# Attention into a mixture of experts: one group's keys and queries loaded in two halves of the heads, six dummy matmuls fewer, and an uneven last output

## The chip, the cores and the metric

The kernel runs on one core of a Trainium2 chip. The time is device microseconds of one launch, as the median of several runs of the same program. The kernel before took 399.28 us (median of 4 runs, 398.71 to 399.73). A change of less than about 0.2% of that, 0.8 us, is treated as no change.

## The reference

```
# attention: B=4, H=8, S=768, D=64; heads 0, 2, 6 are "retrieval" heads
scores = q @ k^T / sqrt(D)
causal mask for retrieval heads; the others see the first 4 keys and a window of 64 keys
a = exp(scores) / (sum + 1e-9)
x = (a @ v), heads side by side, as [B*S, H*D] = [3072, 512]

# four experts, all applied to every row: w1 [4, 512, 1024], w2 [4, 1024, 512]
p = domain_probs / (sum + 1e-9)
out = sum over e of p[:, e] * (relu(x @ w1[e]) @ w2[e])       # [3072, 512], float32
```

All inputs are float32 in the chip's main memory. The kernel computes in float16 with float32 sums.

## The kernel before, in words

**Groups and units.** The 3072 rows are cut into 8 groups of 384 rows: one batch entry has two of them (c = 0 and c = 1). A group's attention makes `xT[g]`, its rows transposed, as four tiles of 128 features (`ct` = 0 to 3, two heads in each). `PLACE` puts head h into tile h % 4, upper or lower half. Then come four units, one for each expert e. A unit has a first layer (32 matmuls on L895: eight output tiles `ft`, each a sum over the four `ct`), a Relu for each `ft` on ScalarE (L908), and a second layer (24 matmuls on L919: three row tiles j, each a sum over eight `ft`), which VectorE scales by p and adds into `acc` (L931, L935).

**What sets the order.** The order on every engine is the order in which the program is written out; nothing is rearranged. While the units of group g are written out, steps of the attention of group g + 1 are slipped between them by the loop at the end of the kernel. It counts planned nanoseconds: attention of group 1 begins when the units of group 0 have `spent` more than `begin` = 1.15 units, and is then spread up to `end`. One unit is 10380 planned nanoseconds. In group 0 a first-layer step counts 0.6 of its time and a second-layer step 1.4, so the first layer of expert 1 begins at about 1.0 units.

**Group 0** has no earlier units to hide behind. Its attention runs first, in the first 22.4 us, with float32 transposes, and TensorE waits for other engines and loads in it. `warm_up` puts dummy matmuls on zeros into such waits (L388). Heads 5 and 7 come last. The last dummies, ten of 256 columns, stand ahead of the value matmuls of head 7. The first unit starts right behind these. For group 0 it takes the tiles in the order `cts` = (0, 2, 1, 3): tile 1 holds heads 1 and 5, tile 3 heads 3 and 7.

**Group 1** is loaded by `load_triples` into `k16` and `qt16`, one DMA for all eight heads of the keys and one for the queries. TensorE transposes both, two heads at a time: `transposes(hp)` is six matmuls for the queries and six for the keys (L516), each a step of its own in the loop. Pairs hp = 0 and 1 (heads 0 to 3) come before the scores, hp = 3 (heads 6, 7) behind the scores of heads 0 and 2, and hp = 2 (heads 4, 5) behind those of heads 1 and 3. From group 2 on, the transposes are done by DMA.

**The loads.** Nearly all loads of the first 65 us are issued by GpSimd (POOL): they convert float32 to float16 on the way. POOL works in program order. `landed(x)` is a tiny copy that makes POOL wait until a transfer has arrived. The order in the stretch that changes is: both halves of w1(1), wait for w1(0), k, q, wait for w2(0), w2(1), wait for q, the values of the three retrieval heads (`vR`), w1(2), wait for w2(1), two other heads' values (`vS`), w2(2), three more, wait for w1(2), w1(3), w2(3). The DMAs that POOL issues take eight semaphores in turn; each first waits until the one eight places before it has landed.

**The end.** The last row tile of the last expert is computed by `last_tile` in two parts of 256 columns, so that the first part is on its way out (issued by SyncE, SP) while the second is computed (its output is issued by ScalarE, ACT).

Of the kernel before, what the change touches and what calls it, by code (L numbers as in the profile page):

```python
# [17 lines left out]
def kernel(  # L18
# [33 lines left out]
    nc = tc.nc  # L52
    P = 128
    B, H, S, D = q.shape
    E, DM, F = moe_w1.shape
    CH = 3 * P
    NCH = S // CH
    N = B * S
    HP = H // 2
# [9 lines left out]
    RH = [h for h in range(H) if RETR[h]]  # L69
# [80 lines left out]
    def half(u):  # L150
        return slice(u * D, (u + 1) * D)
# [5 lines left out]
    def own_v(h):  # L157
        return half(PLACE[h][1])
# [10 lines left out]
    def v_tiles(b, c, h):  # L169

        if RETR[h]:
            return vR[b % 2][:, 3 * c : 3 * c + 3, RH.index(h), :]
        if b:
            return windows(vSf, c)[:, :, SH.index(h), :]
        return vS[:, c, :, SH.index(h), :]
# [10 lines left out]
    def rows_of(x, b, h, c):  # L186
        return x[b, h, c * CH : (c + 1) * CH, :].rearrange("(j p) d -> p j d", p=P)

    def tiles_of(x, b, h, c):
        return x[b, h, c * CH : (c + 1) * CH, :].rearrange("(t r) d -> r t d", r=TK)  # L190

    def windows_of(x, b, h, c):

        assert b > 0
        first = ((b * H + h) * S + c * CH - WO) * D
        return bass.AP(x.tensor, x.offset + first, [[D, P], [WQ * D, WT], [1, D]])
# [10 lines left out]
        q16[b, c] = att.tile([P, 3, H, D], FP16, name="q16", bufs=2)  # L207
        load_by_rows(q, q16[b, c], b, c)

    def load_triples(x, dst, b, c):  # L210

        gp.dma_start(
            out=dst.rearrange("p h j d -> p h (j d)"),
            in_=x[b, :, c * CH : (c + 1) * CH, :].rearrange(
                "h (p j) d -> p h (j d)", j=3
            ),
        )
# [47 lines left out]
    def load_v(b, c, heads):  # L265
        for h in heads:
            t = v_tiles(b, c, h)
            if RETR[h]:
                gp.dma_start(out=t[:, :, 0:D], in_=rows_of(v, b, h, c))  # L269
            elif b:  # L270
                gp.dma_start(  # L271
                    out=t[:, :, own_v(h)], in_=windows_of(v, b, h, c)
                )
            else:
                gp.dma_start(  # L275
                    out=t[R0:P, :, own_v(h)],
                    in_=tiles_of(v, b, h, c),
                )
# [18 lines left out]
    def load_w1(e, f0, f1):  # L297
        x = moe_w1[e].rearrange("(u c d) f -> u d c f", u=2, c=DMP)
        for u in range(2):
            gp.dma_start(  # L300
                out=w1sb[half(u), e * DMP : (e + 1) * DMP, f0:f1],
                in_=x[u, :, :, f0:f1],
            )
# [47 lines left out]
    for h in range(H):  # L351
        if h == 2:
            nc.sync.dma_start(
                out=v_s32, in_=v[0, :, 0:NS, :].rearrange("h r d -> r h d")
# [13 lines left out]
        eng = nc.scalar if h < HP else nc.sync  # L368
        eng.dma_start(out=q32[:, :, h, :], in_=rows_of(q, 0, h, 0))
    nc.sync.dma_start(  # L370
        out=probs, in_=moe_domain_probs.rearrange("(t p) e -> p t e", p=P)
# [14 lines left out]
    def warm_up(ps, n, cols):  # L386
        for _ in range(n):
            nc.tensor.matmul(  # L388
                out=ps[:, 0:cols], lhsT=warm[:, 0:P], rhs=warm[:, 0:cols],
                start=True, stop=True,  # L390
            )
# [63 lines left out]
    k16 = att.tile([P, H, 3, D], FP16, name="k16", bufs=1)  # L455
    qt16 = att.tile([P, H, 3, D], FP16, name="q16", bufs=2)

    def landed(x):

        gp.tensor_copy(out=seen, in_=x)  # L460

    def w1_of(e):
        return w1sb[D : D + 1, e * DMP, 0:1]

    def w2_of(e):
        return w2sb[0:1, e * FTP, 0:1]

    load_w1(1, 0, F)
    landed(w1_of(0))
    load_triples(k, k16, 0, 1)  # L470
    load_triples(q, qt16, 0, 1)
    landed(w2_of(0))
    load_w2(1)
    landed(qt16[0:1, 0, 0, 0:1])
    load_v(0, 1, RH)
    load_w1(2, 0, F)
    landed(w2_of(1))
    load_v(0, 1, SH[:2])
    load_w2(2)
# [12 lines left out]
    def mm_ns(cols):  # L492
        return cols / 2.4 + 2.5

    def attention(b, c):
        g = b * NCH + c
# [212 lines left out]
        def values(h):  # L709
            if RETR[h]:  # L710
                yield from values_r(h)
                return
            ct, u = PLACE[h]
            if first and u == 1:
                ps = pO.tile([P, 512], FP32, name="pO", bufs=2)
            else:
                ps = pV.tile([P, 512], FP32, name="pV", bufs=2)
            if first:
                warm_up(ps, {3: 4, 4: 4, 5: 6, 7: 10}.get(h, 0), 256)
            work = []  # L720
            for es, parts in es_of[h]:
                for t, o, q0, nq in parts:
                    work.append((es, t, o, q0, nq))
            ns = 0
            for n, (es, t, o, q0, nq) in enumerate(work):
                nc.tensor.matmul(  # L726
                    out=ps[:, q0 : q0 + nq],
                    lhsT=v_tile(b, c, h, t),
                    rhs=es[:, o : o + nq],
                    start=(n == 0),  # L730
                    stop=(n == len(work) - 1),
                    skip_group_check=True,
                )
                ns += mm_ns(nq)
                if ns > 300 and n < len(work) - 1:
                    yield ns
                    ns = 0

            r, o = half(u), half(1 - u)
            pair = first and h in (3, 4)  # L740
            if not pair or u == 0:
                rc_of[0] = att.tile([P, CH], FP32, name="rc", bufs=4)
            rc = rc_of[0]
            nc.scalar.activation(  # L744
                out=rc[r, :], in_=ps[o, 0:CH], func=AF.Ln, bias=eps[o, :]
            )

            def scale(r=r, ps=ps):
                nc.vector.tensor_tensor(  # L749
                    out=xT[g][r, ct, :], in0=ps[r, 0:CH], in1=rc[r, :], op=ALU.mult  # L750
                )

            if not pair:
                nc.scalar.activation(out=rc[r, :], in_=rc[r, :], func=AF.Exp, scale=-1.0)  # L754
                later(scale)
            elif u == 0:
                scale_of[0] = scale
            else:
                nc.scalar.activation(out=rc, in_=rc, func=AF.Exp, scale=-1.0)
                later(scale_of[0])  # L760
                later(scale)

            yield ns + (600.0 if g == 1 else 0.0)
# [92 lines left out]

    def last_tile(e, nt, hs, acc):

        for n, eng in enumerate((nc.sync, nc.scalar)):
            cols = slice(n * DM // 2, (n + 1) * DM // 2)  # L860
            ps = pV.tile([P, 512], FP32, name="pV", bufs=2)
            for ft in range(FTP):
                nc.tensor.matmul(
                    out=ps[:, 0 : DM // 2],
                    lhsT=hs[:, ft, 2 * P : 3 * P],
                    rhs=w2sb[:, e * FTP + ft, cols],
                    start=(ft == 0),
                    stop=(ft == FTP - 1),
                )
            nc.vector.scalar_tensor_tensor(  # L870
                out=acc[:, cols], in0=ps[:, 0 : DM // 2],
                scalar=p_sb[:, nt, e : e + 1], in1=acc[:, cols],
                op0=ALU.mult, op1=ALU.add,
            )
            eng.dma_start(out=out[nt * P : (nt + 1) * P, cols], in_=acc[:, cols])


    acc = {}
# [88 lines left out]
    UNIT = FTP * DMP * mm_ns(CH) + 3 * FTP * mm_ns(DM)  # L967
    for g in range(G):
        nxt = g + 1
        n_units = len(units[g])  # L970
        att_steps = iter(())
        if nxt < G:
            att_steps = attention(nxt // NCH, nxt % NCH)
        loads(g + 2)

        begin = {0: 1.15, 1: 1.0}.get(g, 0.0) * UNIT
        end = {0: 3.5}.get(g, 0.90 * n_units) * UNIT

        att_ns = 3500.0 if nxt % NCH == 0 else 5600.0
        if nxt < NCH:  # L980
            att_ns += 1100.0 + HP * 3 * 400.0 + NSH * 600.0
        spent = 0.0
        done = 0.0
        to_transpose = g + 2 < G
        for ns, share in moe_steps(units[g]):

            spent += ns * (share if g == 0 else 1.0)
            tick(ns)
            if to_transpose and spent > {0: 0.9, 1: 0.75}.get(g, 0.5) * n_units * UNIT:
                dma_transposes(*divmod(g + 2, NCH))  # L990
                to_transpose = False
            while done < (spent - begin) / (end - begin) * att_ns:
                step = next(att_steps, None)
                if step is None:
                    break
                done += step
                tick(step)
        for ns in att_steps:
            tick(ns)
        tick(LAG)  # L1000
# [35 lines left out]
```

The softmax here doesn't subtract the row's maximum and nothing guards it: scores larger than these inputs give would overflow.

## Time and profile before

| | |
|---|---|
| median of 4 runs | 399.28 us |
| the profiled execution: its own time, its span | 399.16 us, 397.4 us |
| TensorE (PE) busy | 389.0 us, 98% of the span |
| ScalarE, VectorE, GpSimd busy | 55%, 39%, 36% |
| granted TensorE clock, mean | 0.998 |
| TensorE idle just before it, longest: values of head 5 (load of vS) | 1.02 us |
| the same: second layer of expert 1 (load of w2) | 0.82 us |
| the same: values of head 6 (ScalarE's exp) | 0.76 us |
| POOL's wait for q of group 1 | 7.7 us |

How to read it: the profile is of one execution. Times run from the span's start. A line of the timeline gives the start, the length, the engine, the line of the kernel, the operation with the tiles that it writes and reads, the shape and the count; in brackets stands the idle time of the engine before it and what ended that. In the answers by windows each engine has its busy time and, in parentheses, its number of instructions; then come the granted clock (1.00 is full), the mean busy share of the 16 DMA engines, and GB/s. TensorE's matmuls are pipelined, so the end of one lies behind the start of the next; start-to-start times are the safer measure.

### The profile page before, as it was taken

The page shows a single profiled execution, that of the slowest core. Times are in us where ns is not written, and L with a number is a line of the kernel's source. Part 1 is how long each engine was busy: PE and PEld are TensorE (multiplying, and loading weights), DVE is VectorE, ACT ScalarE, POOL GpSimd, SP SyncE. Part 2 cuts the span into 40 slices and gives each one's busy share as a digit, 9 for nine tenths or more (in the row PEclk, how much of TensorE's full clock was granted, in tenths as well). Part 3 has the DMA queues.
Part 4 walks back from the last instruction along what each step waited for, and adds up shares of the span by engine and source line. Part 5 has one row for each costly group of instructions (what it writes and reads, how often), then busy time and mean ns, then how long its engine had stood idle before and what let it go on. Part 6 is the DMA issues. An engine that isn't in the chain of part 4 may idle for free.

```text
span 397.4 us, 7140 instructions
## 1 busy us (share of the span) xinstructions
PE 389.0 (98%) x2829; PEld 221.7 (56%) x2829; DVE 156.4 (39%) x344; ACT 219.2 (55%) x468; POOL 143.6 (36%) x184
## 2 busy tenths in 40 slices
PE   8899999999999999999999999999999999999996
PEld 5754566555555555555555555555555555555553
DVE  7734765324442234434332333433443223422222
ACT  3754569444766546655764446745564456853331
POOL 8833795908907806900049202940000000000000
PEclk9999999999999999999999999999999999999999
DMA  9999999999999999960779958990472000020002
GB/s 169 162 207 190 172 197 168 146 193 135 117 179 164 121 150 113 150 80 12 140 83 178 59 97 120 112 152 12 86 114 83 2 12 0 11 79 2 0 2 80
DMA packets 166133, 42.23 MB, mean 106 GB/s; under 512 B 156396, under 2 KB 161108, under 8 KB 166100
## 3 DMA queue, kind: packets, MB, share of 16 engines
q0 software_dynamic: 102656, 20.98, 63.1%
q1 hardware_dynamic: 61700, 20.27, 27.0%
q10 hardware_dynamic: 1744, 0.52, 0.6%
q8 instruction: 22, 0.36, 0.4%
q14 instruction: 11, 0.09, 0.1%
HBM read 43.57 MB, written 6.29 MB: 125 GB/s over the span
## 4 chain that ended last, share of the span: by engine, by line
PE 77%; DMA 15%; POOL 6%; issue 1%; DVE 0%; POOLq 0%
PE pA L895 35%; PE pO L919 35%; DMA w1sb<-in_moe_w_dram 4%; DMA w2sb<-in_moe_w_dram 4%; PE pA L614 4%; DMA q<-in_q_dram 3%; DMA kR<-kRr 2%; POOL vR L269 2%; PE pV L726 1%; PE pV L662 1%; DMA vS<-in_v_dram 1%; POOL w1sb L300 1%; POOL vS L275 1%; POOL vS L326 0%; POOL q L201 0%
## 5 line engine op out<-in xcount | busy, mean ns | idle before, releaser
L895 PE MATMUL pA<-xT,w1sb 128*128 128x384 f16 x1024 | 185.9, 326 | 0.1
L919 PE MATMUL pO<-w2sb,hs 128*128 128x512 f16 x760 | 179.0, 379 | 0.8 <-DMA w2sb<-in_moe_w_dram 0.8
L908 ACT ACTIVATE hs<-pA 128x384 f16<-128x384 f32 x256 | 122.0, 492 | 94.8 <-PE pA L895 89.5
L895 PEld LDWEIGHTS <-w1sb 128*128 128x128 f16 x1024 | 95.9, 98 | 59.6 <-issue 0.5
L919 PEld LDWEIGHTS <-hs 128*128 128x128 f16 x760 | 70.8, 98 | 73.9 <-DMA w2sb<-in_moe_w_dram 1.2
L632 ACT ACTIVATE es<-pA 128x384 f16<-128x384 f32 (+2 forms) x122 | 60.0, 511 | 53.6 <-PE pA L614 52.3
L935 DVE SCALAR_TENSOR_TENSOR acc<-pO,p_sb,acc 128x512 f32<-128x512 f32 x71 | 53.3, 751 | 71.7 <-PE pO L919 71.3
L227 POOL DMA_DIRECT2D kSr<-in_k_dram x30 | 30.1, 1008 | 31.9 <-DMA kS<-kSr 21.8
L223 POOL DMA_DIRECT2D kRr<-in_k_dram x18 | 14.2, 786 | 68.5 <-DMA kR<-kRr 68.4
L749 DVE TENSOR_TENSOR xT<-pV,rc 64x384 f16<-64x384 f32 x37 | 20.5, 554 | 32.0 <-ACT rc L754 24.3
L271 POOL DMA_DIRECT2D vS<-in_v_dram x30 | 30.6, 1030 | 0.0
L931 DVE TENSOR_SCALAR acc<-pO,p_sb 128x512 f32<-128x512 f32 x24 | 18.0, 751 | 28.8 <-PE pO L919 28.6
L636 DVE TENSOR_TENSOR es<-es,mC 128x256 f16<-128x256 f16 (+1 forms) x42 | 10.9, 259 | 45.3 <-ACT es L632 44.3
L744 ACT ACTIVATE rc<-pV,eps 64x384 f32<-64x384 f32 x37 | 21.3, 576 | 12.0 <-PE pV L726 11.5
L614 PE MATMUL pA<-qT,kR 128*128 128x384 f16 (+2 forms) x120 | 24.5, 279 | 0.7 <-ACT qT L525 0.4
L754 ACT ACTIVATE rc<-rc 64x384 f32<-64x384 f32 x38 | 19.8, 521 | 1.2
L269 POOL DMA_DIRECT2D vR<-in_v_dram x24 | 19.3, 806 | 0.4 <-issue 0.3
L636 DVE TENSOR_TENSOR es<-es,mW 128x384 f16<-128x384 f16 x30 | 10.7, 358 | 16.9 <-ACT es L632 16.8
L614 PEld LDWEIGHTS <-kR 128*128 128x128 f16 x120 | 11.4, 98 | 10.7 <-DVE kR L532 0.7
L726 PEld LDWEIGHTS <-vS 128*128 128x128 f16 x255 | 13.4, 98 | 6.9 <-DMA vS<-in_v_dram 1.3
L662 PEld LDWEIGHTS <-es 128*128 128x128 f16 x252 | 13.2, 97 | 7.2 <-ACT es L632 0.9
L614 PEld LDWEIGHTS <-kS 128*128 128x128 f16 x255 | 13.3, 98 | 6.6
(102 smaller groups left out, 190.5 us busy)
## 6 DMA issues: line engine op xcount, KB each, us to landing
out_dram<-acc SPq DMA_DIRECT2D x23, 256.0 KB
w1sb<-in_moe_w_dram POOLq DMA_DIRECT2D x8, 512.0 KB, 9.9
w2sb<-in_moe_w_dram POOLq DMA_DIRECT2D x4, 1024.0 KB, 13.3
kSr<-in_k_dram POOLq DMA_DIRECT2D x30, 112.0 KB, 3.7
vS<-in_v_dram POOLq DMA_DIRECT2D x30, 112.0 KB, 5.5
q<-in_q_dram POOLq DMA_DIRECT2D x18, 128.0 KB, 4.3
vR<-in_v_dram POOLq DMA_DIRECT2D x24, 48.0 KB, 4.6
kRr<-in_k_dram POOLq DMA_DIRECT2D x18, 48.0 KB, 3.5
```

The lines of the kernel that those rows point to most:

```text
L227: gp.dma_start(out=kSr[:, :, SH.index(h), own(h)], in_=windows_of(k, b, h, c),)
L269: gp.dma_start(out=t[:, :, 0:D], in_=rows_of(v, b, h, c))
L271: gp.dma_start(out=t[:, :, own_v(h)], in_=windows_of(v, b, h, c))
L614: nc.tensor.matmul(out=ps[:, o : o + nq], lhsT=key_tile(b, c, h, t), rhs=qTs[b, c][:, hp, q0 : q0 + nq], start=(n == 0 or not first), stop ...
L632: nc.scalar.activation(out=es[:, 0:cols], in_=ps[:, 0:cols], func=AF.Exp, scale=SC)
L636: nc.vector.tensor_tensor(out=es[:, o0:o1], in0=es[:, o0:o1], in1=m[:, mo : mo + o1 - o0], op=ALU.mult,)
L744: nc.scalar.activation(out=rc[r, :], in_=ps[o, 0:CH], func=AF.Ln, bias=eps[o, :])
L749: nc.vector.tensor_tensor(out=xT[g][r, ct, :], in0=ps[r, 0:CH], in1=rc[r, :], op=ALU.mult)
L895: nc.tensor.matmul(out=pss[ft][:, 0:CH], lhsT=w1sb[:, e * DMP + ct, ft * P : (ft + 1) * P], rhs=xT[g][:, ct, :], start=(n == 0), stop=(n = ...
L908: nc.scalar.activation(out=hs[:, ft, :], in_=ps[:, 0:CH], func=AF.Relu)
L919: nc.tensor.matmul(out=ps_o, lhsT=hs[:, ft, j * P : (j + 1) * P], rhs=w2sb[:, e * FTP + ft, :], start=(ft == 0), stop=(ft == FTP - 1),)
L935: nc.vector.scalar_tensor_tensor(out=acc[nt], in0=ps_o, scalar=p_ap, in1=acc[nt], op0=ALU.mult, op1=ALU.add,)
```

## The change

There are four edits.

1. `load_triples` takes a range of heads. Heads 0 to 3 of k and q are loaded where all eight were; w1(2) is issued right after the wait for q (which now waits for the first half), then the values of heads 0 and 2, then heads 4 to 7 of k and q, then the values of head 6.
2. Attention of group 1 begins at 1.05 units instead of 1.15.
3. The dummies ahead of head 7's values are 4 instead of 10.
4. The last tile is computed in parts of 384 and 128 columns instead of 256 and 256.

```diff
-    def load_triples(x, dst, b, c):
+    def load_triples(x, dst, b, c, h0, h1):
 
         gp.dma_start(
-            out=dst.rearrange("p h j d -> p h (j d)"),
-            in_=x[b, :, c * CH : (c + 1) * CH, :].rearrange(
+            out=dst[:, h0:h1, :, :].rearrange("p h j d -> p h (j d)"),
+            in_=x[b, h0:h1, c * CH : (c + 1) * CH, :].rearrange(
                 "h (p j) d -> p h (j d)", j=3
             ),
         )
...
     load_w1(1, 0, F)
     landed(w1_of(0))
-    load_triples(k, k16, 0, 1)
-    load_triples(q, qt16, 0, 1)
+    load_triples(k, k16, 0, 1, 0, HP)
+    load_triples(q, qt16, 0, 1, 0, HP)
     landed(w2_of(0))
     load_w2(1)
     landed(qt16[0:1, 0, 0, 0:1])
-    load_v(0, 1, RH)
     load_w1(2, 0, F)
+    load_v(0, 1, RH[:2])
+    load_triples(k, k16, 0, 1, HP, H)
+    load_triples(q, qt16, 0, 1, HP, H)
+    load_v(0, 1, RH[2:])
     landed(w2_of(1))
...
-                warm_up(ps, {3: 4, 4: 4, 5: 6, 7: 10}.get(h, 0), 256)
+                warm_up(ps, {3: 4, 4: 4, 5: 6, 7: 4}.get(h, 0), 256)
...
-        for n, eng in enumerate((nc.sync, nc.scalar)):
-            cols = slice(n * DM // 2, (n + 1) * DM // 2)
+        for c0, c1, eng in ((0, 3 * P, nc.sync), (3 * P, DM, nc.scalar)):
+            cols = slice(c0, c1)
...
-                    out=ps[:, 0 : DM // 2],
+                    out=ps[:, 0 : c1 - c0],
...
-                out=acc[:, cols], in0=ps[:, 0 : DM // 2],
+                out=acc[:, cols], in0=ps[:, 0 : c1 - c0],
...
-        begin = {0: 1.15, 1: 1.0}.get(g, 0.0) * UNIT
+        begin = {0: 1.05, 1: 1.0}.get(g, 0.0) * UNIT
```

In the order of TensorE's instructions this moves the transposes of group 1 forward. In the first layer of expert 1, the queries of heads 0 and 1 come behind 8 matmuls instead of 20, the keys behind 16 instead of 24, and the queries of heads 2 and 3 behind 28 instead of in the second layer; the pairs for heads 2, 3 and for heads 6, 7, which stood together, now have second-layer or first-layer matmuls between queries and keys. The queries of heads 6 and 7 come behind 16 matmuls of that second layer, where they came behind 20.

## The prediction

> **What bounds the kernel now.** I read the page's first part, then TensorE's timeline around the changed stage, then the chain of waits and the waits there, then the last microseconds.
>
> ```profile
> PE 389.0 (98%) x2829; PEld 221.7 (56%) x2829; DVE 156.4 (39%) x344; ACT 219.2 (55%) x468; POOL 143.6 (36%) x184
> ```
>
> TensorE is busy for 389.0 of 397.4 us, so an edit pays only by what it takes out of or puts into TensorE's row, or the tail. 8.4 us are idle in all, and no edit can return more.
>
> TensorE's timeline (start, length, instructions, idle before):
>
> ```profile
> 20.64 0.42 PE L726 MATMUL pO<-es,vS 128*128 128x160 f16 x4 [1.02 <-DMA vS<-in_v_dram]
> 21.07 1.25 PE L388 MATMUL pO<-warm 128*128 128x256 f16 x10
> 22.16 0.41 PE L726 MATMUL pO<-es,vS 128*128 128x160 f16 x4
> 22.41 5.75 PE L895 MATMUL pA<-xT,w1sb 128*128 128x384 f16 x32
> ...
> 33.17 3.41 PE L895 MATMUL pA<-xT,w1sb 128*128 128x384 f16 x20
> 36.52 0.36 PE L516 MATMUL pV<-ident,q 128*64 128x128 f16 x6
> 36.81 0.82 PE L895 MATMUL pA<-xT,w1sb 128*128 128x384 f16 x4
> 37.56 0.36 PE L516 MATMUL pV<-ident,k 128*64 128x128 f16 x6
> 37.85 1.47 PE L895 MATMUL pA<-xT,w1sb 128*128 128x384 f16 x8
> 40.15 1.04 PE L919 MATMUL pO<-w2sb,hs 128*128 128x512 f16 x4 [0.82 <-DMA w2sb<-in_moe_w_dram]
> ```
>
> Here: the dummies (L388, x10), and the one stall in the changed stage, at 40.15, for w2(1). Lengths contain pipeline fill, so I price by start-to-start pitch: L895 0.1625 us (32 in 5.20), L919 0.216. The eight L895 from 37.85 are issued by 39.15, so the stall costs 40.15 - 39.15 = 1.00 us.
>
> The chain of waits, and who waits for q:
>
> ```profile
> 21.61 13.47 DMA q<-in_q_dram
> 35.66 2.27 POOL vR L269 x3
> 38.58 8.00 DMA w1sb<-in_moe_w_dram
> ```
> ```profile
> POOL seen L460 <- DMA q<-in_q_dram: 7.7, 1, 7.7
> ```
>
> The loads on POOL's queue land in order of issue, one behind the other. By their issue times plus "DMA to landing": second half of w1(1) 30.95, k 33.05 (20.73 + 12.3), q 35.08, w2(1) 40.10 (26.58 + 13.5), three vR 40.46, 40.79, 41.15, second half of w1(2) 46.57. So k costs the queue 2.10 us, q 2.03, w2(1) 5.02, a vR 0.35, w1(2) 5.42, though w1(1), behind a full queue, took 4.95 (26.00 to 30.95).
>
> **The change, part by part.**
>
> *Halves.* Half of k and q is (2.10 + 2.03) / 2 = 2.07 us of queue, so q's first half lands near 33.0 and w2(1) near 38.05, before TensorE can ask for it. The stall goes: -1.00 us. POOL's wait for q ends 2 us earlier too, so w1(2) is issued from about 33.7 instead of 37.92 and is queued well before w2(1) ends.
>
> What is late next is the second half. It stands behind w2(1), w1(2) and two vR: 33.0 + 5.02 + 4.95 + 0.70 + 2.07 = 45.75 with w1(2) at the full-queue price; at the price of the row (5.42) 46.2. The queue's dips bear on which:
>
> ```profile
> 39.00:40.00 1.00, 0.33 (x3) 0.00 (x0) 0.66 (x1) 0.82 (x3) 0.20 (x1) 1.00 1.17 112
> 41.00:42.00 1.00, 1.00 (x15) 0.57 (x15) 0.48 (x1) 0.00 (x0) 1.00 (x2) 1.00 0.75 111
> ```
>
> The last column is GB/s, against 204 at 35.0 to 37.5. The first dip falls behind w1(2)'s late issue and should go; the second I cannot explain. I take the middle, 46.0.
>
> *The earlier start (1.15 to 1.05 units).* The order of the changed program puts q's transposes of heads 0 and 1 behind 8 L895 instead of 20, about 34.5 us; q's first half is there since 33.0. Before the first L919 of expert 1 now stand three transpose blocks instead of two. A block of six (L516) costs 0.29 us of its own and 0.10 for getting into it (36.52 less 33.17 + 3.25), 0.39 alone; two in a row take 0.57 (41.01 to 41.58). The order before has six insertions, after has eight, since two pairs are split: 2 x 0.19 = +0.38 us.
>
> Now the walk to the second half. 33.17 + 5.20 + 3 x 0.39 = 39.54: first L919. Then, in the new order, 16 L919 (3.45), the k block (0.39), and 14 score matmuls (7 in 0.82 at 43.31 to 44.13, 6 in 0.66, one of 0.16: 1.64): 45.02, and with the 0.10 the transposes of heads 6 and 7 ask for q at 45.1. Before, the same transposes ran at 46.77, with q landed since 35.08: eleven microseconds of cover become none. Stall: 46.0 - 45.1 = +0.9 us, with 45.75 and 46.2 as near ends (+0.65, +1.1). It blocks TensorE in order: the k block, the L919 of expert 1 and all scores stand behind it. The far ends: nothing, were the dips all gone and the queue 0.65 us quicker; and +3.5 us, if w1(2) lands no earlier than before (46.57 + 2.07 = 48.6).
>
> *What POOL is moved past.* Two more DMA instructions, 0.90 us each at most (the whole k took that to issue), and POOL is waiting 2 us less. POOL's loads take eight semaphores in turn, and each waits for the load eight places before; what follows shifts by two places: w2(2) now waits for w1(2)'s second half (about 43), w1(3) for q's second half (46.0, before: issued at 47.16). The queue holds work throughout, so what follows lands as before: two vR at 44 against a use near 48. 0; at worst one issue late, +0.3.
>
> A rule of the Trainium skill ("DMA: Bandwidth & Descriptors", Bandwidth, and the section on one DMA's anatomy) speaks against splitting: about 2 us fixed per DMA, batch to 1 MiB. Row: the vR, 48 KB each, landed 0.33 and 0.36 us apart, so in this queue the fixed part is hidden. By the rule, as an estimate, two more DMAs would be up to 4 us of queue and a stall near 5 us.
>
> *Six dummies fewer.* 6 x 0.109 = 0.65 us of TensorE time leave, but what comes behind them is late:
>
> ```profile
> 22.26 0.56 DVE L749 TENSOR_TENSOR xT<-pO,rc 64x384 f16<-64x384 f32 x1 [0.43 <-ACT rc L754]
> 23.77 0.56 DVE L749 TENSOR_TENSOR xT<-pO,rc 64x384 f16<-64x384 f32 x1 [0.95 <-ACT rc L754]
> ```
>
> The first is xT of head 5, ended at 22.82. The third L895 (ct = 1) reads it and started at 22.87, already 0.14 late. Head 5's values waited for a load (20.64, above), not for dummies. So the dummies' time becomes idle: 0. Bounds: -0.65 if that third matmul did not wait; above, the first 16 L895 at half clock, 16 x 0.1625 = +2.6. Rows against the latter: from 17.40 to 20.80 TensorE was busy 1.62 of 3.40 us and the granted clock stayed 1.00; the stretch 19.50 to 22.90 now falls from 2.38 to about 1.7. I take 0.
>
> The skill's rule ("TensorE: Matmul & The Clock Gate", Part 1): half clock after an idle window of about 3.4 us. If it struck, one such window at half clock would cost some 1.7 us (an estimate by that page); the rows say 0.
>
> *The last tile.* The sixteen matmuls keep their columns. The first DVE step grows to 384 columns: from 751 ns at 512 and 484 at 256, 0.62 us; the second shrinks to 0.35.
>
> ```profile
> 393.61 0.33 SPq L875 DMA_DIRECT2D out_dram<-acc  x1
> 393.80 0.48 DVE L870 SCALAR_TENSOR_TENSOR acc<-pV,p_sb,acc 128x256 f32<-128x256 f32 x1 [0.39 <-PE pV L863]
> 394.32 0.36 ACTq L875 DMA_DIRECT2D out_dram<-acc  x1
> ```
>
> The first part's matmuls end 0.43 later (393.32), DVE runs 393.36 to 393.97, SP issues near 394.17 instead of 393.61; DVE's second step waits for its first, ends at 394.33, ACT issues at 394.36 instead of 394.32. So neither issue is earlier, and SP now carries 192 KB half a microsecond later. From ACT's issue to the span's end 3.08 us: if SP's takes its place, 394.17 + 3.08 + 64 KB at 204 GB/s (0.31) = 397.56, +0.16; if ACT's share runs wholly behind it +0.5; if the smaller last part lands quicker -0.15. I take +0.15.
>
> *Later.* TensorE waits once more, 0.13 us at 85.95, for a key transpose that SP issues behind an output that TensorE makes; a shift of a few tenths moves both. 0, or -0.13 if loads end earlier.
>
> **Sum.** -1.00 + 0.38 + 0.90 + 0 + 0.15 = +0.43; with -0.1 for the wait at 85.95, about +0.3 us. The profiled execution took 399.16 us (span 397.4), 0.12 under the median 399.28. 399.28 + 0.3 = 399.6. A measurement of this kernel tells about 0.2%, 0.8 us, from no change, so this is no change.
>
> **Rivals.**
> - *The second half is in time.* Needs q by 45.1. For it: w1(2) queued early, both dips gone. Against: 45.75 is already the full-queue price. Then -1.00 + 0.38 - 0.1 + 0 to 0.15 gives -0.6 to -0.75: about 398.5, near the bound; with a tail gain past it. Chance 0.25.
> - *Slower: the second half lands past 46.4.* Mechanism: TensorE stands in L516 for q while expert 1's L919 wait behind it. Price is landing less 45.1; from 46.4 on the sum is over +0.8. For it: the second dip stays, or engines of the queue finish unevenly; against: w1(2)'s earlier issue. At 46.6 to 47.5: +1.0 to +1.9, so 400.3 to 401.2. Chance 0.28.
> - *The halves do not part:* if the first transposes waited for the whole tile, 46.0 - 34.5 = 11.5 us lost. Against: head 1's values ran at 13.42, head 5's load into the same tile vS landed at 20.6. Chance 0.01.
> - *Clock lost to the missing dummies:* +2.6 as bounded above; no row shows the clock under 1.00. 0.03.
>
> Forecast, within 0.8 us: 0.43. Its upper edge (stall 1.3) adds 0.04 to slower; of the first rival 0.16 is past the bound. Slower 0.36, faster 0.16, same 0.48. The range: 398.5 (the first rival's middle) to 400.6 (a stall of 1.9) leaves about 0.2 out.
>
> **What would show it.** Right: no idle before expert 1's first L919 (about 39.5); a new idle before L516 for q near 45, 0.5 to 1.2 us, put down to DMA q; idle of 0.6 to 0.8 near 22; SP's last issue near 394.2 if nothing else shifted. Wrong: no idle at that L516 (then the queue was quicker than 45.1), an idle over 1.3, a granted clock under 1.00 near 22 to 26, or L895 at 22.4 moving earlier as a whole.

## The result, and the profile after

| | before | after |
|---|---|---|
| median | 399.33 us (70 runs) | 400.15 us (47 runs) |
| after / before | | 1.0020, 95% interval 1.0013 to 1.0027 |
| profiled execution: its own time, its span | 399.16, 397.4 us | 399.59, 397.8 us |

The change costs 0.8 us (0.5 to 1.1): a small loss, clear of the noise, and just about the 0.2% under which a change was to count as none. The forecast was 399.6 in 398.5 to 400.6: the direction was right, the size 0.55 us low. Lines move down by three: L895, L919, L516 and L614 of before are L898, L922, L519 and L617 here.

TensorE's work first (busy time, share of the span, instructions):

```profile
PE 388.8 (98%) x2823; PEld 220.9 (56%) x2823; DVE 156.2 (39%) x344; ACT 219.6 (55%) x468; POOL 144.2 (36%) x186
```

Six instructions and 0.2 us fewer on TensorE, two more on POOL, and yet a longer span: the time is in waits. TensorE's timeline of after, in the stretch shown of before:

```profile
21.01 0.49 PE L898 MATMUL pA<-xT,w1sb 128*128 128x384 f16 x2
21.90 5.29 PE L898 MATMUL pA<-xT,w1sb 128*128 128x384 f16 x30 [0.40 <-DVE xT L752]
...
32.20 1.46 PE L898 MATMUL pA<-xT,w1sb 128*128 128x384 f16 x8
33.60 0.36 PE L519 MATMUL pV<-ident,q 128*64 128x128 f16 x6
...
37.93 0.82 PE L898 MATMUL pA<-xT,w1sb 128*128 128x384 f16 x4
38.59 1.03 PE L922 MATMUL pO<-w2sb,hs 128*128 128x512 f16 x4
...
43.69 0.54 PE L617 MATMUL pA<-qT,kR 128*128 128x128 f16 x3
45.52 0.36 PE L519 MATMUL pA<-ident,q 128*64 128x128 f16 x6 [1.29 <-DMA q<-in_q_dram]
...
86.30 0.39 PE L617 MATMUL pA<-qT,kR 128*128 128x128 f16 x2 [0.64 <-DMA kR<-kRr]
```

The stall for w2(1) before expert 1's second layer (0.82 us before) is gone: the first L922 at 38.59 follows the L898 with no bracket. Two new brackets stand further on, for the second half of q (1.29) and for group 2's keys (0.64). The same line of before follows an idle time of 0.13 only:

```profile
85.95 0.39 PE L614 MATMUL pA<-qT,kR 128*128 128x128 f16 x2
```

One thing must be taken out first. Expert 1's first matmul starts at 32.20, 0.97 earlier than before's 33.17. That is no work of the change: its distance from the landing of head 5's values is the same, and that load landed at 19.62 here and at 20.59 before. Over the twelve profiles with this order of group 0's loads that start scatters from 32.20 to 33.88. So I count from that start on:

| | before | after | difference |
|---|---|---|---|
| span | 397.37 | 397.81 | +0.44 |
| start of expert 1 | 33.17 | 32.20 | -0.97 |
| from there to the instruction ahead of group 2's first score | 52.32 | 53.14 | +0.82 |
| from that instruction to the score (wait for keys) | 0.46 | 0.96 | +0.50 |
| score to first matmul of the last tile | 305.90 | 305.90 | 0.00 |
| from there to the end | 5.52 | 5.60 | +0.09 |

The rows below the start sum to +1.41 and, with -0.97, give the +0.44. The medians say +0.8; one pair of profiles has the sign and the places, not the exact size. The rows are not independent either: a wait for a load eats part of what an earlier start had won.

The queue on POOL, first the two lines of before, then after:

```profile
35.20 0.18 POOL L460 COPY seen<-q 1x1 f16<-1x1 f16 x1 [7.75 <-DMA q<-in_q_dram]
42.04 0.91 POOL L306 DMA_DIRECT2D w2sb<-in_moe_w_dram  x1
```

```profile
32.75 0.18 POOL L460 COPY seen<-q 1x1 f16<-1x1 f16 x1 [5.70 <-DMA q<-in_q_dram]
33.20 1.24 POOL L300 DMA_DIRECT2D w1sb<-in_moe_w_dram  x2 [0.28 <-issue]
40.43 0.67 POOL L275 DMA_DIRECT2D vS<-in_v_dram  x1 [1.02 <-DMA w1sb<-in_moe_w_dram]
42.98 0.90 POOL L306 DMA_DIRECT2D w2sb<-in_moe_w_dram  x1 [1.88 <-DMA w1sb<-in_moe_w_dram]
```

The wait for q ended 2.45 us earlier, as meant. But the issue of w2(2) now waits 1.88 us for w1(2)'s second half, the load eight places ahead, and stands 0.94 later than before. It landed at 54.80 instead of 53.85, w1(3) at 61.52 instead of 60.36, w2(3) at 66.44 instead of 65.47: the large loads behind it are about a microsecond late.

The transpose that brings group 2's keys was itself not issued later; first before, then after:

```profile
78.27 1.47 SPq L259 DMA_TRANSPOSE kR<-kRr  x1
```

```profile
78.08 1.84 SPq L259 DMA_TRANSPOSE kR<-kRr  x1
```

The score that waits for it started 7.68 us behind that issue in before and 8.22 in after. Late loads do not explain this by themselves: in e6 below, whose loads of that time are those of before (w2(3) landed at 65.52), it was 8.95; in e2, whose loads are at least as late as after's (67.13), the score waited for nothing and came 7.40 behind.

### The profile page after: what moved, and what is told of

The parts are those of the page before. It is cut to its first block, busy times and chain, and to the rows that moved or that the text cites. A ratio compares the mean times of both kernels' runs of the same rounds, so it can differ in the third digit from the quotient of the medians.

```text
span 397.8 us, 7128 instructions
## 1 busy us (share of the span) xinstructions
PE 388.8 (98%) x2823; PEld 220.9 (56%) x2823; DVE 156.2 (39%) x344; ACT 219.6 (55%) x468; POOL 144.2 (36%) x186
## 4 chain that ended last, share of the span: by engine, by line
PE 77%; DMA 15%; POOL 6%; issue 1%; DVE 0%; DVEq 0%; POOLq 0%
PE pA L898 35%; PE pO L922 35%; DMA w2sb<-in_moe_w_dram 5%; DMA w1sb<-in_moe_w_dram 4%; PE pA L617 4%; DMA q<-in_q_dram 3%; DMA kR<-kRr 2%; PE pV L729 1%; PE pV L665 1%; POOL vS L275 1%; POOL vR L269 1%; DMA vS<-in_v_dram 1%; POOL q L201 1%; POOL w1sb L300 1%; POOL vS L326 0%
## 5 line engine op out<-in xcount | busy, mean ns | idle before, releaser
L898 PE MATMUL pA<-xT,w1sb 128*128 128x384 f16 x1024 | 185.9, 326 | 0.5 <-DVE xT L752 0.4
L922 PE MATMUL pO<-w2sb,hs 128*128 128x512 f16 x760 | 179.4, 379 | 0.0
L898 PEld LDWEIGHTS <-w1sb 128*128 128x128 f16 x1024 | 95.9, 98 | 60.4 <-issue 0.9
L922 PEld LDWEIGHTS <-hs 128*128 128x128 f16 x760 | 70.9, 98 | 72.5 <-ACT hs L911 0.7
L617 PE MATMUL pA<-qT,kR 128*128 128x384 f16 (+2 forms) x120 | 24.3, 278 | 1.3 <-DMA kR<-kRr 0.6
L617 PEld LDWEIGHTS <-kR 128*128 128x128 f16 x120 | 11.3, 98 | 11.2 <-DMA kR<-kRr 1.0
L617 PEld LDWEIGHTS <-kS 128*128 128x128 f16 x255 | 13.1, 98 | 6.2 <-DVE kS L559 0.2
```

The lines of the kernel that those rows point to most:

```text
L617: nc.tensor.matmul(out=ps[:, o : o + nq], lhsT=key_tile(b, c, h, t), rhs=qTs[b, c][:, hp, q0 : q0 + nq], start=(n == 0 or not first), stop ...
L898: nc.tensor.matmul(out=pss[ft][:, 0:CH], lhsT=w1sb[:, e * DMP + ct, ft * P : (ft + 1) * P], rhs=xT[g][:, ct, :], start=(n == 0), stop=(n = ...
L922: nc.tensor.matmul(out=ps_o, lhsT=hs[:, ft, j * P : (j + 1) * P], rhs=w2sb[:, e * FTP + ft, :], start=(ft == 0), stop=(ft == FTP - 1),)
```

## The experiments

Theory A puts the loss on TensorE's path: q's second half is asked for earlier than it lands, behind w1(2). The rivals put it elsewhere: into the arrival of group 2's keys (theory B), the loads behind the second half (theory C of e5 and e10), the dummies (rival C of e2) or the tail. Ratios are to the kernel before, run on the same chip. The edits are to the kernel after where nothing else is said; line numbers differ by up to three between the kernels.

**e1: the halves, with the attention of group 1 at its old place.**

```diff
-        begin = {0: 1.05, 1: 1.0}.get(g, 0.0) * UNIT
+        begin = {0: 1.15, 1: 1.0}.get(g, 0.0) * UNIT
```

> The changed kernel with attention of group 1 beginning at 1.15 units again (edit 2 undone, the rest kept). Theory A (the loss is TensorE standing for q's second half, about 1.3 us, plus 0.4 us for two more insertions of transposes, less the 1.0 us of the w2(1) wait that is gone): q of heads 6 and 7 is asked for 0.5 us later counted from the first matmul of expert 1, and the two insertions are gone, so the wait falls to 0 to 0.8 us and the time is 0.2 to 1.0 us under before (ratio 0.9975 to 0.9995). Theory B (the time is set by the arrival of group 2's transposed keys at about 86 us, and the changed order of loads made the queue 1 us later; what TensorE does before that is hidden): the time stays where the changed kernel is, 0.5 to 0.8 us over before (1.0012 to 1.002), and TensorE's idle time ahead of the first score of group 2 grows to 1.0 to 1.8 us.

Measured: 398.58 us, ratio 0.9991 (0.9979 to 1.0002). TensorE's waits from 15 to 90 us:

```profile
PE pA L617 <- DMA kR<-kRr: 0.9, 1, 0.9
...
PE pO L922 <- DMA w2sb<-in_moe_w_dram: 0.5, 1, 0.5
PE pA L519 <- DMA q<-in_q_dram: 0.3, 1, 0.3
```

The loss goes with the begin, as A had it. But there is no gain to speak of either, although the stall of 1.00 for w2(1) is gone in this kernel too. The lines say where it went: 0.3 for q's second half, 0.5 for w2(2), issued at 43.33 and landed at 54.93, and 0.9 for the keys. The profile is of an execution 0.58 us over the median, so these waits are seen, not priced. A stall removed in an early stage met three later loads that were no earlier.

**e2: ten dummies again.**

```diff
-                warm_up(ps, {3: 4, 4: 4, 5: 6, 7: 4}.get(h, 0), 256)
+                warm_up(ps, {3: 4, 4: 4, 5: 6, 7: 10}.get(h, 0), 256)
```

> The changed kernel with ten dummies ahead of head 7's values again (edit 3 undone). Theories A and B both say no difference from the changed kernel: the third matmul of expert 0 waits for xT of head 5 with or without them (ratio to before 1.0015 to 1.0025), and the idle time of 0.40 us near 21.5 us turns into dummies. Rival C (the missing dummies cost clock or start): back to before, 1.000.

Measured: 400.27 us, ratio 1.0027 (1.0015 to 1.0039), no better than after. Timeline of e2, and then of e12 below, which has four dummies:

```profile
21.66 1.26 PE L388 MATMUL pO<-warm 128*128 128x256 f16 x10
22.75 0.41 PE L729 MATMUL pO<-es,vS 128*128 128x160 f16 x4
23.00 1.76 PE L898 MATMUL pA<-xT,w1sb 128*128 128x384 f16 x9
```

```profile
21.28 0.49 PE L895 MATMUL pA<-xT,w1sb 128*128 128x384 f16 x2
22.40 2.27 PE L895 MATMUL pA<-xT,w1sb 128*128 128x384 f16 x13 [0.63 <-DVE xT L749]
```

With ten there is no bracket in front of the first layer, with four there is one of 0.63, the dummies' time (0.65) turned into idle. The third first-layer matmul, which reads xT of head 5, started 2.28 us after head 5's values landed in both (23.47 after 21.19; 22.40 after 20.12).

**e3: the last tile in equal parts again.**

```diff
-        for c0, c1, eng in ((0, 3 * P, nc.sync), (3 * P, DM, nc.scalar)):
+        for c0, c1, eng in ((0, 2 * P, nc.sync), (2 * P, DM, nc.scalar)):
```

> The changed kernel with two last parts of 256 columns again (edit 4 undone). The prediction put the tail at +0.15 us, so 0.15 us less than the changed kernel: ratio to before 1.0015 or so, within noise of the changed kernel. If the tail cost its upper bound, 0.5 us, the ratio is about 1.0007. From the first matmul of the last tile to the end of the span it should take 5.5 us again (before 5.55; changed 5.6).

Measured: 399.44 us, ratio 1.0007 (0.9991 to 1.0022). The interval holds after's 1.0020 and 1, so the ratio decides nothing. The profiles say more: from the last tile's first matmul to the end it took 5.42 us on average in the three with equal parts (5.52, 5.38, 5.37), 5.53 in the eleven with 384 and 128 (5.37 to 5.67). The uneven cut costs about 0.1 us, though the two groups overlap.

**e4: the loads whole again, the rest of the change kept.**

```diff
-    load_triples(k, k16, 0, 1, 0, HP)
-    load_triples(q, qt16, 0, 1, 0, HP)
+    load_triples(k, k16, 0, 1, 0, H)
+    load_triples(q, qt16, 0, 1, 0, H)
...
+    load_v(0, 1, RH)
     load_w1(2, 0, F)
-    load_v(0, 1, RH[:2])
-    load_triples(k, k16, 0, 1, HP, H)
-    load_triples(q, qt16, 0, 1, HP, H)
-    load_v(0, 1, RH[2:])
```

> The changed kernel with k and q of group 1 in one DMA each and the old order of loads (edit 1 undone), attention still beginning at 1.05 units. Theory A: TensorE waits about 0.6 us for q at its first transposes (35.1 against 34.5), after which w2(1) is in time; two more insertions 0.4 us; so 0 to 0.3 us over before, plus the tail (ratio 1.000 to 1.0012). Theory B: the queue is that of before, the keys of group 2 arrive as before, so the same as before within 0.3 us; the two do not part here, but if this kernel is as slow as the changed one (1.002) the loss is not in the halves at all.

Measured: 399.13 us, ratio 0.9996 (0.9984 to 1.0008). In its profile the first transposes wait 1.83 us for the whole q (landed 35.72), well over the 0.6 that A gave. That profile took 53.74 us on the path that took 52.32 before, so by it the kernel ought to lose; the median does not show that, and why it does not is open. What the ratio does show: the earlier begin alone costs nothing that can be measured.

**e5: q's second half right behind the first.** Both second halves are issued behind the wait for the first, ahead of vR and w1(2).

```diff
     landed(qt16[0:1, 0, 0, 0:1])
-    load_w1(2, 0, F)
-    load_v(0, 1, RH[:2])
     load_triples(k, k16, 0, 1, HP, H)
     load_triples(q, qt16, 0, 1, HP, H)
-    load_v(0, 1, RH[2:])
+    load_v(0, 1, RH)
+    load_w1(2, 0, F)
```

> The changed kernel with the second half of k and q issued right behind the wait for the first half, ahead of the three vR and w1(2) (the rest kept, attention at 1.05 units). Then q's second half lands near 40 us instead of 45.5, and w2(2) has to wait only for q's second half, so it is issued near 41.5 instead of 43.0. Theory A (TensorE's wait for q makes the loss): the idle time of 1.29 us ahead of the transposes of heads 6 and 7 is gone, the two insertions of 0.19 us stay, w2(1) is in time: 0.3 to 0.6 us under before, less what the keys of group 2 take back near 86 us, so ratio 0.9985 to 1.000. Theory C (the loss is w2(2) issued 1 us late, which lands 11.4 to 12.1 us after its issue in all six kernels so far, and pushes every later load by 1 us): w2(2) lands near 53.3 and the keys of group 2 are there at 85.9 or earlier; also 1.000 or under. If the time stays at 1.002, both fall and the loss is in the dummies or the tail.

Measured: 398.68 us against 399.87 of before on that chip, ratio 0.9968 (0.9955 to 0.9981): faster. Its timeline:

```profile
38.52 0.82 PE L897 MATMUL pA<-xT,w1sb 128*128 128x384 f16 x4
39.18 1.03 PE L921 MATMUL pO<-w2sb,hs 128*128 128x512 f16 x4
...
44.28 0.54 PE L616 MATMUL pA<-qT,kR 128*128 128x128 f16 x3
44.76 0.36 PE L518 MATMUL pA<-ident,q 128*64 128x128 f16 x6
...
84.73 0.38 PE L616 MATMUL pA<-qT,kR 128*128 128x128 f16 x2
```

No bracket is left: not for w2(1), not for q (landed at 39.74, asked at 44.76), not for the keys. POOL could issue w2(2) at 40.03, and it landed at 52.55, 2.3 us before after's. From expert 1's start to group 2's first score it took 51.94 us, against 54.10 in after and 52.77 before. The 2.16 us to after agree with the ratios (0.0052 of 400 us is 2.1). With the halves and the early begin both kept, the order of loads alone turns the loss into a gain. It moves two things at once, q's second half and the issue of w2(2), so e5 does not tell which of them counts.

**e6: the same with begin at 1.15.** e5 with e1's edit.

> The same as the run with the second half issued early, with attention of group 1 at 1.15 units, so without the two additional insertions. Counted from the first matmul of expert 1, TensorE reaches the second layer of expert 2 0.38 us earlier than with 1.05 units. If nothing takes it back the ratio is 0.9965 to 0.998; if the keys of group 2 bind at 85.9 us it is 0.9985 to 1.000, with 0.8 to 1.3 us of idle time put down to their transpose.

Measured: 398.69 us, ratio 0.9975 (0.9957 to 0.9993), no better than e5, so the 0.38 us of the split transposes did not come back as a gain. Its profile, an execution of 400.14 us and so 1.45 over its own median, shows two waits that can take it:

```profile
PE pA L616 <- DMA kR<-kRr: 1.4, 1, 1.4
PE pA L897 <- DMA w1sb<-in_moe_w_dram: 1.1, 1, 1.1
```

TensorE was ready for expert 2 at about 46.8 and began it at 47.88, because w1(2) was whole only at 47.75. In e5 it was whole at 46.23, issued 0.14 us earlier; with that landing nothing would have waited here, so this wait is the scatter of one execution.

**e7 and e9: group 2's keys transposed earlier.** SP issues them ahead of the first output instead of behind it, once in after (e7) and once, as a control, in before (e9).

```diff
-            if to_transpose and spent > {0: 0.9, 1: 0.75}.get(g, 0.5) * n_units * UNIT:
+            if to_transpose and spent > {0: 0.85, 1: 0.75}.get(g, 0.5) * n_units * UNIT:
```

> The changed kernel with the key and query transposes of group 2 issued by SP ahead of the first output of group 0 instead of behind it (they begin when the planned time passes 0.85 of group 0's units instead of 0.9). They are then bound by their loads alone, and the keys should arrive 0.5 to 2 us before 86. If part of the changed kernel's loss is taken at that place (0.64 us of idle time in its profile), the ratio falls from 1.002 to about 1.0005 to 1.001. If TensorE's own path decides (the 0.64 being what that run had won at its start, where the load of head 5's values landed 1 us earlier than in the profile of before), the ratio stays at 1.0015 to 1.002.

> The kernel before with one edit: the transposes of group 2's keys and queries are issued ahead of the first output of group 0 (0.85 instead of 0.9). A control for the same edit on the changed kernel, which brought it from 1.002 to 0.9989. If the arrival of the keys binds only in the changed kernel, this one gains at most the 0.13 us that TensorE waited there before: 0.9995 to 1.000. If it binds in most executions of the kernel before as well, 0.997 to 0.999, and then the place takes back part of any gain made ahead of it, in both kernels alike.

Measured: e7 399.04 us, ratio 0.9989 (0.9976 to 1.0002); e9 398.59 us, ratio 0.9977 (0.9962 to 0.9991). No profile of the two shows a wait for keys; e7's shows the wait for q unchanged in kind, 1.04 us. So the keys are worth about a microsecond (1.2 us from after to e7, 0.9 from before to e9), but in before as well: they are no cost that the change alone brought. With them out of the way e7 stands 0.0012 (0.5 us) over e9, with intervals that overlap. One point stays open: the profile of before shows only 0.13 us of idle for the keys, and e9's profile takes the same 52.77 us from expert 1's start to the first score. What the control gained, its median shows and its profile does not.

**e8 and e11: the better orders together.** e8 is e6, with e7's edit and the values of heads 5 and 7 of group 0 ahead of expert 0's w1. e11 is e8 with w1(2) ahead of the three vR.

```diff
-    load_v(0, 0, [2, 1, 3, 4, 6])
+    load_v(0, 0, [2, 1, 3, 4, 6, 5, 7])
...
-    load_v(0, 0, [5, 7])
...
     load_triples(q, qt16, 0, 1, HP, H)
-    load_v(0, 1, RH)
     load_w1(2, 0, F)
+    load_v(0, 1, RH)
```

> A version meant to beat both: first and second halves in a row ahead of w1(2), attention at 1.15 units, the transposes of group 2 ahead of the first output, and the values of heads 5 and 7 of group 0 loaded ahead of w1(0). The wait for w2(1) (1.0 us) and the wait for head 5's values (0.9 to 1.8 us of idle time in the profiles so far, of which ScalarE and VectorE behind it leave 0.5 to 1.0 to win) should go, and the keys should not bind: 397.4 to 398.3 us, ratio 0.995 to 0.9975. If the queue of loads alone sets the arrival of group 2's keys, 0.9985 and an idle time of 1 to 2 us near 85 us.

> The version that was meant to beat both (second halves ahead of w1(2), 1.15 units, early transposes of group 2, values of heads 5 and 7 of group 0 ahead of w1(0)), with w1(2) ahead of the three vR. Its profile had 0.33 us of idle time for w1(2) (landed 46.76) left at 46.9; w1(2) then lands near 45.7 and that goes. 0.3 us under the version with vR ahead: ratio 0.9945 to 0.9965. If the ratio stays at 0.9962 the keys or the start bind instead.

Measured: e8 398.24 us, ratio 0.9962 (0.9947 to 0.9976), with 0.33 us left for w1(2); e11 397.37 us, ratio 0.9955 (0.9940 to 0.9969), the lowest ratio of the case, not parted from e8's, and faster than both kernels. Its ten runs lie between 397.20 and 399.00. Timeline and wait in e11:

```profile
21.18 5.29 PE L896 MATMUL pA<-xT,w1sb 128*128 128x384 f16 x30 [0.23 <-DVE xT L750]
26.84 5.35 PE L920 MATMUL pO<-w2sb,hs 128*128 128x512 f16 x24 [0.38 <-DMA w2sb<-in_moe_w_dram]
```

```profile
PE pO L920 <- DMA w2sb<-in_moe_w_dram: 0.9, 2, 0.5
```

Head 5's values land at 14.42 and are waited for no more; the first layer waits only 0.23 us, for VectorE's xT and not for a load. What is left are two short waits, for w2(0) and for w2(1).

**e10: w2(2) issued ahead of the two vS.** In after, so that w2(2) no longer waits for w1(2)'s second half.

```diff
     landed(w2_of(1))
-    load_v(0, 1, SH[:2])
     load_w2(2)
+    load_v(0, 1, SH[:2])
     load_v(0, 1, SH[2:])
```

> The changed kernel with w2(2) issued ahead of the values of the heads 1 and 3 instead of behind them, so that the load it has to wait for by its semaphore is w2(1) (landed 38.1) and not w1(2)'s second half (42.7). The wait for q's second half (1.0 to 1.3 us) and the two insertions stay. Theory C (w2(2)'s late issue is the loss): w2(2) lands near 51 instead of 54.8, w2(3) near 65 instead of 66.4, the keys are there in time and the time is back at 0.999 to 1.000. Theory A (TensorE's path): 1.0015 to 1.002 as the changed kernel. Both by half: about 1.0005 to 1.001.

Measured: 398.82 us, ratio 0.9995 (0.9975 to 1.0016). The 1.26 us for q stay, the wait for keys is gone from its profile, which had started expert 1 at 33.66, 1.46 us later than after's. What the queue moved from 45 to 47 us (the last column is GB/s), in after and then in e10:

```profile
45.00:47.00 2.00, 1.48 (x16) 0.70 (x16) 0.80 (x1) 0.29 (x2) 1.96 (x5) 1.00 1.17 116
```

```profile
45.00:47.00 2.00, 0.74 (x7) 0.23 (x7) 1.18 (x3) 1.71 (x5) 1.99 (x3) 1.00 1.31 191
```

After runs thin there, two microseconds behind the late issue of w2(2); e10, which issued it at 39.23, does not, and has w2(2) at 53.16 although its q half landed 1.4 us later than after's. Part of e10's 191 is its own q half, which was still landing then. The landing says it better: w2(2) came 1.64 us before after's. So the late issue was felt by the load. The ratio points the same way, but its interval holds after's as well: how much of the 0.8 us the late loads make is not settled.

**e12: only the dummies and the tail, in the kernel before.**

```diff
-                warm_up(ps, {3: 4, 4: 4, 5: 6, 7: 10}.get(h, 0), 256)
+                warm_up(ps, {3: 4, 4: 4, 5: 6, 7: 4}.get(h, 0), 256)
...
-        for n, eng in enumerate((nc.sync, nc.scalar)):
-            cols = slice(n * DM // 2, (n + 1) * DM // 2)
+        for c0, c1, eng in ((0, 3 * P, nc.sync), (3 * P, DM, nc.scalar)):
+            cols = slice(c0, c1)
...
```

> The kernel before with the changed kernel's dummies (4) and last tile (384 and 128 columns) alone, the loads and the begin of before. The prediction priced these at 0 and +0.15 us: ratio 1.000 to 1.0005. If the loss sits in them, 1.001 to 1.002.

Measured: 398.85 us, ratio 0.9994 (0.9982 to 1.0007). These two edits are not the loss. All six kernels below have both of them, so they make a table of the other two:

| loads of group 1 | begin 1.15 | begin 1.05 |
|---|---|---|
| whole | 0.9994 (e12) | 0.9996 (e4) |
| halves, the second behind w1(2) | 0.9991 (e1) | 1.0020 (after) |
| halves, the second behind the first | 0.9975 (e6) | 0.9968 (e5) |

Neither edit loses alone: the intervals of e1 and e4 end at 1.0002 and 1.0008, after's begins at 1.0013. The loss needs the early begin and the late second half together, and it turns into a gain when the second half comes early.

## Why the prediction was right, and where its sum was short

The call of no change came out right at its very border. That the pair of profiles has +0.44 us and the sum +0.43 is luck: the +0.44 holds 0.97 of an earlier start that no term had, and 0.50 for the keys.

- **w2(1), -1.00: right.** It landed at 38.08 (38.05 forecast), q's first half at 32.62 (33.0). No idle stood before the first L922.
- **Insertions, +0.38: right.** A block still takes 0.10 to get into and 0.29 of its own, and eight stand where there were six.
- **When q's second half is asked for: right.** In e5, where nothing waited, the transposes started 11.97 us after expert 1's start (44.76 less 32.79); the walk gave 11.95.
- **When it lands, and the wait of 0.9: right in the mean, short for this profile.** It landed at 45.48, half a microsecond before the forecast 46.0, but 13.28 us after expert 1's start, where the sum had 12.83 (46.0 less 33.17). The start follows head 5's load, which lands when it lands, and the queue does not move fully with it. In the five profiles with this order (after, e2, e3, e7, e10) the idle was 1.29, 0.15, 1.08, 1.04 and 1.26, 0.96 on average (in e3 the trace names ScalarE as the releaser, but q had landed only 0.04 us before). Here the step cost 1.35 from start to start (13.32 less 11.97) instead of 0.9, in the band that the prediction had put at the edge of slower. An estimate from one execution should have carried that scatter.
- **What POOL is moved past, 0: this step failed.** It named the wait of w2(2) for w1(2)'s second half and its time (about 43; it was 42.98), and then said that the queue holds work throughout. It did not: w2(2) landed 8.4 us after the load in front of it (46.37), where the row for such a load had 5.0, and the large loads from there on came 0.95 to 1.20 us late. The premise failed in before's own rows, where w2(2) landed 6.80 us after the load in front (53.85, 47.05). In both kernels it landed 11.8 us after its issue, so the later issue was passed on whole. The price in after is hidden for w2(2) itself (landed 54.80, used at 55.40) and seen in e1 (0.5 us).
- **The wait for keys, 0 or -0.13: failed.** In this pair it was +0.50. It varies by execution: e2, with the same loads, had no wait for keys, e3 1.08. What lengthens the transpose from issue to use, at most 7.40 us in e2 and 8.95 in e6, is open.
- **Dummies, 0: right** (e2, e12). On the clock, the Trainium skill ("TensorE: Matmul & The Clock Gate", Part 1) has it halved after an idle window of about 3.4 us. In a stretch of that length in e3, which has four dummies and the latest values, TensorE was busy for 1.60 of 3.40 us and the clock (the third number from the right) held, as the row below shows. A stretch of such length with TensorE wholly idle stands only behind its last matmul, where nothing waits for it: in before that matmul ended at 393.8 and the granted clock was 0.52 from 396.00 to the end, which makes the mean of 0.998; in after it stayed 1.00 for the 3.7 us to the end.

```profile
20.10:23.50 3.40, 1.60 (x17) 1.27 (x18) 1.10 (x2) 1.65 (x3) 1.68 (x3) 1.00 1.25 206
```

- **Tail, +0.15: right in kind**, 0.09 in the pair and about 0.1 over all profiles. In after, DVE's two steps run back to back and the parts go out 0.27 us apart (before: 0.71), SP's three quarters of the tile among the last:

```profile
393.71 0.88 DVE L873 SCALAR_TENSOR_TENSOR acc<-pV,p_sb,acc 128x384 f32<-128x384 f32 x2 [0.55 <-PE pV L866]
394.35 0.33 SPq L878 DMA_DIRECT2D out_dram<-acc  x1
394.62 0.37 ACTq L878 DMA_DIRECT2D out_dram<-acc  x1
```

- **The rule against splitting.** The second halves of k and q landed at 44.33 and 45.48, 1.15 us apart at 192 KB each. The four halves took 2.08 and 2.17 us of the queue, the two whole loads 4.13: two more loads cost it 0.1 us and not 4. The prediction's bound by the rule fell, and its queue price of about 1.03 a half held.

Of the rivals, the second half in time is what e5 is, not what after is. The slower one has the forecast's own mechanism, TensorE standing in the transposes of heads 6 and 7, with a later landing. In this profile it is at its edge: 13.28 us behind before's start of 33.17 is 46.45, and it was to decide from 46.4. Over the five profiles the forecast's 0.9 stands. How the 0.8 us of the medians divide between this wait and the late loads and keys stays open.

## What to carry to other kernels

When a load is split so that its first part comes early, write down when each part is used, and give the second part its place in the queue by that time; here moving it ahead of a weight load of 1 MB and two small loads turned a loss of 0.2% into a gain of 0.3%. A stall taken out early is only worth what the next loads allow: list the next three loads with landing and use before counting it. And price a race between an engine and a queue over several executions, since the two scatter against each other by more than the effect.

## What was not expected of the hardware

- The same load of head 5's values, issued in the same place, landed between 19.62 and 21.29 us in the twelve profiles with its old order. With it the whole kernel starts earlier or later, by 1.7 us from the earliest to the latest; the runs of before spread over 2.7 us (398.18 to 400.90).
- A 1 MB load issued 0.94 us later, while the queue still held other loads, landed 0.95 later; issued 3.75 us earlier (e10 against after), it landed 1.64 earlier.
- From group 2's first score to the last tile the kernel took 305.88 to 305.91 us in all fourteen profiles, so all that changes here is in the first 90 us and the last 6.
